# Attention and a gated MLP in one kernel: the late head pairs' scores as three products of split queries and keys

## The chip, the cores and the metric

The kernel runs on one core of a Trainium2 chip. The metric is the device time of one execution in microseconds (us). Times inside an execution come from one profiled run, counted from the start of its span.

## The reference

Eight batches of eight heads, 576 positions, 64 values per head. The attention mask is by blocks of 64: a query sees all keys of its own and of earlier blocks. The heads of a batch side by side are the 512 columns of the MLP's input, 4608 tokens in all.

```python
scores = 1/sqrt(64) * q @ k.T          # per batch and head, 576 x 576
scores = where(block_i >= block_j, scores, -1e9)
attn = exp(scores - max(scores)); attn /= sum(attn) + 1e-9
x = (attn @ v).transpose(0, 2, 1, 3).reshape(4608, 512)
h = x @ w_in                           # 512 x 2048
out = (h / (1 + exp(-1.702 * h))) @ w_out   # 2048 x 512
```

Everything comes in and goes out in float32; queries and keys are scaled so that the scores are spread widely.

## The kernel before, in words

**Attention.** Two heads make a pair; there are 32 pairs, four to a batch. A pair's two heads lie on partitions 0 to 63 and 64 to 127, so their score matmuls stand in different halves of the TensorE rows. `load` (L279) brings a pair's queries and keys into one tile, `raw`; `prep` (L303) turns both with two VectorE transposes into `qk` and, once `raw` is read, starts the load of the pair that follows. The 576 queries are five chunks (0 to 4) that see 64, 192, 320, 448 and 576 keys. `score` (L316) multiplies chunks 3 and 0, 2 and 1 in one block of four widths (448, 64, 320, 192) for each head; chunk 4 (384 and 192 wide) is multiplied behind the attention-times-values matmuls of the pair before, in `av` (L499 to L515). Each score is one float32 matmul (L340, L504, L511), all of them issued by the helper `mm` (L110). VectorE then adds the mask and takes the maximum (L389), ScalarE exponentiates (L396), GpSimd or VectorE divide by the sum (L415, L417).

**Early and late.** Pairs 0 to 7 are early: their weights are flipped on TensorE (L448). Pairs 8 to 31 are late: VectorE turns 32 x 32 blocks (L424, L429), and sixteen DMAs on the SyncE queue (L436) put the blocks in place. `settle` (L349) runs `prep` of the next pair after the scores of chunk 4.

**The MLP.** It works in tiles of 384 tokens, twelve in all (`moe`, L580). Each factor is a higher part, rounded to the reduced float32 (`F32R`), and a lower part, the rest; a product is three matmuls of parts (L617, L585). For each of 16 slices of the hidden width a tile has 12 matmuls into a bank `hp` (384 columns), the gate (`g`, `gh`, `gl`: L633, L634, L642, L643), and 9 matmuls of the slice before into the banks `acc0` to `acc2` (512 columns each). After the last slice, ScalarE copies each `acc` bank into an `osb` tile (L599), and a DMA on the SyncE queue writes it out (L601). The next tile's first matmul into an `acc` bank waits for the copy of that bank. There are three `osb` buffers.

**Weights.** They come as 64-bit words, and 32 pieces are merged (`begin`, `merge`) into a tile `wm`, of which ScalarE takes the higher part and GpSimd the lower (`split_weights`, L250, the subtraction is helper L84). The last pieces are staged in `osb` buffers and in a buffer tagged `e1`. The last piece is split while pair 7 is worked on.

**Order.** `ORDER` and its kin (L26 to L34) set the order in which a pair's steps are written; `advance` (L663) puts MLP matmuls between them. TensorE runs in just that order. On the other engines the order comes out of priorities. Each engine and the SyncE queue works in order: what waits holds up all behind it.

**Buffers.** A tag with one buffer holds one tile; the next tile of that tag waits until all readers of the old one are done.

Of the kernel before, what the change touches and what calls it, by code (L numbers as in the profile page):

```python
# [10 lines left out]
F32 = mybir.dt.float32  # L11
F32R = mybir.dt.float32r
U32 = mybir.dt.uint32
# [28 lines left out]
def attention_moe_kernel(  # L42
# [9 lines left out]
    nc = tc.nc  # L52
    B, H, S, D = q.shape
    DM, DF = w_in.shape
    P = 128
# [11 lines left out]
    K4 = 384  # L67

    sp = ctx.enter_context(tc.tile_pool(name="sp", bufs=1))
    d2 = ctx.enter_context(tc.tile_pool(name="d2", bufs=2))  # L70
    ps = ctx.enter_context(tc.tile_pool(name="ps", bufs=1, space=PSUM))

    def f(ap):
        return ap.bitcast(F32)

    def early(n):

        return n < 2 * HP
# [4 lines left out]
    def subtract(eng, out, in0, in1):  # L83
        eng.tensor_tensor(out=out, in0=in0, in1=in1, op=ALU.subtract)  # L84
# [3 lines left out]
    turns = {"n": 0, "bank": 0, "experts": False, "late": False}  # L88
# [20 lines left out]
    def mm(**kw):  # L109
        return tc.keep_in_program_order(nc.tensor.matmul(**kw))  # L110
# [14 lines left out]
    WC = 512  # L125
# [4 lines left out]
    def room(tag, shape, dt, name):  # L130
        return d2.tile(shape, dt, tag=tag, name=name, bufs=1)

    home = {}

    def weights(name, g):
# [36 lines left out]
    for i in range(NCH):  # L172
        w, o = BLK * (2 * i + 1), 2 * BLK * i * i
        es.append(flat[:, o : o + 2 * w].rearrange("p (h k) -> p h k", h=2))

    def width(i):
        return BLK * (2 * i + 1)
# [9 lines left out]
    for g in range(NG):  # L187
# [3 lines left out]
        for fc in range(FG):  # L191
            r = (g * FG + fc) * P
# [5 lines left out]
    def load_weights(upto):  # L198
        while conv["loaded"] < min(upto, len(pieces)):
            j = conv["loaded"]  # L200
            if j < 2 * len(places):
                if j % 2 == 0:
                    pair_of[j // 2] = room(places[j // 2], [P, 2, 2 * WC], U32, "words")
                at = [pair_of[j // 2][:, j % 2]]
            else:
                at = [
                    room("e1", [P, WC], U32, "wst") if j % 2 and x
                    else d2.tile([P, WC], U32, tag="osb", name="wst", bufs=3)
                    for x in range(2)
                ]  # L210
            n = 2 * WC // len(at)
            for x, w in enumerate(at):
                d = nc.sync.dma_start(out=w, in_=pieces[j][0][:, x * n : (x + 1) * n])
                if j < 3:
                    tc.keep_in_program_order(d)
            parts[j] = [
                (w.rearrange("p (c t) -> p c t", t=2), slice(x * n // 2, (x + 1) * n // 2))
                for x, w in enumerate(at)
            ]
            conv["loaded"] += 1  # L220
# [3 lines left out]
    bits, whole = {}, {}  # L224
# [48 lines left out]
    raw, qk = {}, {}  # L273
# [21 lines left out]
    def load_v(n):  # L295
        to = values(n)
        for hd, b, h in heads(n):
# [2 lines left out]
            )  # L300
            nc.sync.dma_start(out=to[0:BLK, hd, QC], in_=v[b, h, QC * P : S])

    def prep(n):  # L303

        tag = "e0" if early(n) and n % 2 else "qk"
        qk[n] = d2.tile([P, 2, S], F32, tag=tag, name="qk", bufs=1)
        for x in range(2):
            nc.vector.transpose(out=qk[n][:, x], in_=raw[n][:, x].rearrange("p c d -> p (c d)"))  # L308
        raw.pop(n)
        m = follower(n)  # L310
        if m is not None:
            load(m)
# [3 lines left out]
    def score(n, banks):  # L316

        turns["late"] = not early(n)
        if n not in stats:
            mx = d2.tile([P, NCH + 1, 2], F32, tag="mx", name="mx")  # L320
            sm = d2.tile([P, NCH, 2], F32, tag="sm", name="sm")
            stats[n] = (mx, sm)
        todo = []
        taken = 0
        for chunks in banks:

            part = []
            for lo, hi in ((0, 512),) if width(chunks[0]) <= 512 else ((0, 256), (256, S)):
                ss = []
                for _ in range(2):  # L330
                    taken += 1
                    ss.append(lent_bank() if taken == 1 and turns["late"] else bank())
                c = 0
                for i in chunks:
                    a, z = qrange(i)
                    w = min(hi, width(i)) - lo
                    for hd in range(2):
                        r = slice(hd * D, hd * D + D)

                        mm(  # L340
                            out=ss[hd][:, c : c + w], lhsT=qk[n][r, 0, a : a + P],
                            rhs=qk[n][r, 1, lo : lo + w], start=True, stop=True,
                        )
                        part.append((i, hd, lo, lo + w, ss[hd][0 : z - a, c : c + w]))
                    c += w
            todo.append(sorted(part, key=lambda x: (chunks[::-1].index(x[0]), x[2])))
        settle(n, banks, todo)
# [120 lines left out]
    def av(n):  # L468

        b, h = divmod(n, HP)  # L470
        before_av(n)
        if turns["late"]:
            o0, o = bank(), bank()
            cut = BLK + 2 * P
        else:
            o, o0 = bank(), bank()
            cut = BLK

        def place(q0):
            return (o0, q0) if q0 < cut else (o, q0 - cut)  # L480

        todo = []
        for i in range(1, NCH):
            bk, c = place((i - 1) * P + BLK)
            todo += [(bk, c, P, j, pw[:, :, SLOT[i] + j]) for j in range(i)]
            todo.append((bk, c + BLK, BLK, i, pw[:, 2:4, 9 + i]))
        todo.append((*place(0), BLK, 0, pw[:, 0:2, 10]))

        ends = [[x for x, y in enumerate(todo) if y[0] is bk] for bk in (o0, o)]
        for x, (bk, c, nn, j, w) in enumerate(todo):  # L490
            for hd in range(2):
                mm(
                    out=bk[hd * D : hd * D + D, c : c + nn].rearrange("d (a c) -> d a c", c=32),
                    lhsT=values(n)[:, hd, j], rhs=w[:, :, hd],
                    start=any(x == y[0] for y in ends), stop=any(x == y[-1] for y in ends),
                )
        m = n + 1
        rest = []
        if turns["late"] and m < NPAIR:  # L499
            own = [lent_bank(), bank()]  # L500
            a, z = qrange(4)
            for hd in range(2):
                r = slice(hd * D, hd * D + D)
                mm(  # L504
                    out=own[hd][:, 0:K4], lhsT=qk[m][r, 0, a : a + P],
                    rhs=qk[m][r, 1, 0:K4], start=True, stop=True,
                )
                rest.append((4, hd, 0, K4, own[hd][0 : z - a, 0:K4]))
            for hd, (bk, c) in enumerate(((o0, cut), (o, S - cut))):
                r = slice(hd * D, hd * D + D)  # L510
                mm(  # L511
                    out=bk[:, c : c + S - K4], lhsT=qk[m][r, 0, a : a + P],
                    rhs=qk[m][r, 1, K4:S], start=True, stop=True,
                )
                rest.append((4, hd, K4, S, bk[0 : z - a, c : c + S - K4]))  # L515
        c0 = (b % 2) * S
        nc.scalar.copy(out=xr[:, h, c0 : c0 + cut], in_=o0[:, 0:cut])
        nc.scalar.copy(out=xr[:, h, c0 + cut : c0 + S], in_=o[:, 0 : S - cut])
        nxt = follower(n)
        if nxt is not None:  # L520
            load_v(nxt)
        if rest:
            settle(m, [[4]], [sorted(rest, key=lambda x: x[2])])
# [56 lines left out]
    def moe():  # L580
        prev = None

        def second(state):
            g_hi, g_lo, fc, acc, t = state
            todo = [(c, ga, wb) for c in range(TILES[t][1] // P) for ga, wb in ((g_hi, "woh"), (g_hi, "wol"), (g_lo, "woh"))]  # L585
            if fc < NFC - 1:

                todo.sort(key=lambda x: x[1] is g_lo)
            begun = set()
            for x, (c, ga, wb) in enumerate(todo):  # L590
                last = ga is g_lo
                mm(
                    out=acc[c], lhsT=ga[:, c * P : (c + 1) * P], rhs=weights(wb, fc // FG)[:, fc % FG],
                    start=fc == 0 and c not in begun, stop=fc == NFC - 1 and last,
                )
                begun.add(c)
                if fc == NFC - 1 and last:
                    osb = d2.tile([P, DM], F32, tag="osb", name="osb", bufs=3)
                    nc.scalar.copy(out=osb, in_=acc[c])  # L599
                    r = TILES[t][0] + c * P  # L600
                    nc.sync.dma_start(out=out[r : r + P, :], in_=osb)  # L601
                if x % 3 == 2:
                    yield 650

        for t in range(NT):
# [6 lines left out]
            for fc in range(NFC):  # L612
# [8 lines left out]
                for cnt, (wa, xb, dc) in enumerate(terms):  # L621
                    mm(
                        out=hp[:, 0:tt], lhsT=weights(wa, fc // FG)[:, dc, fs], rhs=xb[:, dc, 0:tt],
                        start=cnt == 0, stop=cnt == 3 * NDC - 1,
# [111 lines left out]
```

## Time and profile before

| | us |
|---|---|
| Median of 3 runs | 1097.73 (1097.12 to 1099.45) |
| The profiled execution | 1097.56 |
| Its span | 1095.8 |
| TensorE matmuls busy | 1063.1 (97% of the span) |
| VectorE, ScalarE, GpSimd busy | 603.6, 499.3, 403.9 |

In a timeline a row is a start, a duration, an engine, a line, an operation and how many of them were merged into it; what stands in brackets is the idle time of the engine before the row and who ended it. PE is TensorE, PEld its weight loads, DVE VectorE, ACT ScalarE, POOL GpSimd, SPq the SyncE queue of DMAs. `bank<-qk` is a score matmul; a float32 matmul leaves two records, so eight records are four matmuls. Matmul durations overlap: what one costs is the distance from its start to the next start.

### The profile page before, as it was taken

How to read it: one execution, taken by the hardware profiler on the slowest of the kernel's cores; microseconds unless marked ns; L12 is line 12 of the kernel's file. 1: busy time of each engine (PE TensorE's matmuls, PEld its weight loads, DVE VectorE, ACT ScalarE, POOL GpSimd, SP SyncE). 2: the span in 40 equal slices, each digit the busy share in tenths (PEclk: the TensorE clock that was granted, in tenths of full speed). 3: DMA queues.
4: the chain of work that ended last, by engine and by line, in shares of the span. 5: the costliest groups of instructions: out<-in, count | busy, mean ns of one | idle time of the engine just before them, and what ended most of it. 6: DMA issues, size and time to landing. Idle time of an engine off the chain costs nothing.

```text
span 1095.8 us, 19944 instructions
## 1 busy us (share of the span) xinstructions
PE 1063.1 (97%) x6960; PEld 913.4 (83%) x6960; DVE 603.6 (55%) x1856; ACT 499.3 (46%) x1321; POOL 403.9 (37%) x509
## 2 busy tenths in 40 slices
PE   6869999999999999999999999999999999999998
PEld 4657777888888888888888888888888888999997
DVE  6786786765655656655655665655656655111111
ACT  5866776533443544533444543443544433322322
POOL 4666565423333333233333332333333233222222
PEclk8979999999999999999999999999999999999999
DMA  8734523433423444342434433233443321200000
GB/s 175 208 92 156 148 63 81 86 90 78 98 67 77 116 88 87 62 99 65 105 78 87 116 73 74 58 98 77 108 95 84 73 77 47 55 30 1 30 1 29
DMA packets 219364, 91.24 MB, mean 83 GB/s; under 512 B 197760, under 2 KB 197760, under 8 KB 219264
## 3 DMA queue, kind: packets, MB, share of 16 engines
q1 hardware_dynamic: 214528, 89.38, 34.5%
q10 hardware_dynamic: 4736, 0.59, 0.3%
q8 instruction: 55, 0.90, 0.3%
q14 instruction: 45, 0.37, 0.1%
HBM read 45.09 MB, written 9.44 MB: 50 GB/s over the span
## 4 chain that ended last, share of the span: by engine, by line
PE 89%; DVE 4%; ACT 2%; issue 2%; DMA 1%; SPq 1%; POOL 1%; POOLq 0%; DVEq 0%; ACTq 0%
PE hp L110 36%; PE acc L110 35%; PE bank L110 17%; PE bank L113 1%; ACT turned L396 1%; DMA raw<-in_k_dram 1%; SPq L290 1%; DVE wm L245 1%; DVE sm L405 1%; DVE qk L308 0%; DVE turned L389 0%; DVE e L389 0%; DMA words<-in_moe_w_out_dram 0%; DVE wm L240 0%; ACT e L396 0%
## 5 line engine op out<-in xcount | busy, mean ns | idle before, releaser
L84 POOL TENSOR_TENSOR gl<-g,gh 128x384 fp32r<-128x384 f32 x192 | 194.8, 1014 | 573.5 <-ACT gh L642 568.3
L634 DVE SCALAR_TENSOR_TENSOR g<-g,hp 128x384 f32<-128x384 f32 x192 | 104.9, 546 | 379.6 <-ACT g L633 379.5
L110 PE MATMUL hp<-xh,wih 128*128 128x384 f32 x768 | 260.6, 339 | 2.9 <-DVE g L634 2.2
L110 PE MATMUL hp<-xh,wil 128*128 128x384 f32 x768 | 258.1, 336 | 0.0
L110 PE MATMUL hp<-xl,wih 128*128 128x384 f32 x768 | 254.1, 338 | 0.1
L633 ACT ACTIVATE g<-hp 128x384 f32<-128x384 f32 x192 | 94.3, 491 | 312.8 <-PE hp L110 299.8
L110 PE MATMUL acc<-woh,gh 128*128 128x512 f32 x576 | 231.6, 402 | 0.0
L110 PE MATMUL acc<-wol,gh 128*128 128x512 f32 x576 | 226.7, 394 | 0.0
L110 PE MATMUL acc<-woh,gl 128*128 128x512 f32 x576 | 168.1, 393 | 0.5 <-POOL gl L84 0.5
L642 ACT CAST gh<-g 128x384 fp32r<-128x384 f32 x192 | 98.5, 513 | 141.0 <-DVE g L634 140.9
L110 PEld LDWEIGHTS hp<-xh,wih 128*128 128x128 f32 x768 | 144.3, 188 | 15.8 <-issue 3.3
L110 PEld LDWEIGHTS hp<-xh,wil 128*128 128x128 f32 x768 | 144.2, 188 | 7.7
L396 ACT ACTIVATE e<-e,mx 64x64 f32<-64x64 f32 (+4 forms) x240 | 131.9, 551 | 28.8 <-DVE mx L389 28.8
L110 PEld LDWEIGHTS hp<-xl,wih 128*128 128x128 f32 x768 | 143.6, 188 | 1.0 <-DVE xl L84 0.9
L110 PE MATMUL bank<-qk 64*128 64x192 f32 (+5 forms) x768 | 122.1, 431 | 13.9 <-DVE qk L308 11.1
L110 PEld LDWEIGHTS acc<-woh,gh 128*128 128x128 f32 x576 | 107.9, 187 | 28.1 <-issue 7.4
L415 POOL TENSOR_TENSOR e<-e,sm 64x64 f32<-64x64 f32 (+1 forms) x192 | 111.7, 611 | 51.7 <-DVE sm L410 40.7
L110 PEld LDWEIGHTS acc<-woh,gl 128*128 128x128 f32 x576 | 107.7, 188 | 25.8 <-POOL gl L84 1.8
L110 PEld LDWEIGHTS acc<-wol,gh 128*128 128x128 f32 x576 | 108.2, 188 | 16.5 <-issue 0.4
L110 PEld LDWEIGHTS bank<-qk 64*128 64x128 f32 x768 | 69.9, 194 | 53.5 <-issue 18.0
L389 DVE CUSTOM_DVE_ANT_0 e<-bank,mask 64x64 f32<-64x64 f32 (+4 forms) x240 | 92.8, 440 | 16.4 <-PE bank L110 15.2
L110 PEld LDWEIGHTS bank<-turned,vp 128*64 128x64 f32 x1800 | 85.4, 137 | 9.6 <-issue 6.6
(50 smaller groups left out, 985.7 us busy)
## 6 DMA issues: line engine op xcount, KB each, us to landing
turned<-turned SPq DMA_DIRECT2D x192, 80.0 KB, 2.1
turned<-turned SPq DMA_DIRECT2D x96, 112.0 KB, 2.2
raw<-in_q_dram SPq DMA_DIRECT2D x128, 72.0 KB, 2.4
out_dram<-osb SPq DMA_DIRECT2D x36, 256.0 KB, 2.2
raw<-in_k_dram SPq DMA_DIRECT2D x120, 72.0 KB, 2.3
turned<-turned SPq DMA_DIRECT2D x96, 88.0 KB, 2.1
words<-in_moe_w_in_dram SPq DMA_DIRECT2D x16, 512.0 KB, 5.7
vp<-in_v_dram SPq DMA_DIRECT2D x60, 128.0 KB, 2.5
```

The lines of the kernel that those rows point to most:

```text
L84: eng.tensor_tensor(out=out, in0=in0, in1=in1, op=ALU.subtract)
L110: return tc.keep_in_program_order(nc.tensor.matmul(**kw))
L113: return tc.keep_in_program_order(nc.tensor.transpose(**kw))
L245: nc.vector.scalar_tensor_tensor(out=z[:, c], in0=w[..., 0], scalar=29, in1=u[:, c], op0=ALU.logical_shift_right, op1=ALU.bitwise_or,)
L290: queue.dma_start(out=raw[n][r : r + 32, x], in_=src[b, h][:, c : c + 32].rearrange("(c p) d -> p c d", p=32),)
L389: nc.vector.tensor_tensor_reduce(out=e[0:m, hd, lo:hi], in0=s, in1=mk, op0=ALU.add, op1=ALU.min, scale=-0.125, scalar=3e38 if lo == 0 else ...
L396: nc.scalar.activation(out=e[0:m, hd], in_=e[0:m, hd], func=AF.Exp, scale=-1.0, bias=mx[0:m, i, hd : hd + 1], accum_out=sm[0:m, i, hd : hd ...
L405: x = nc.vector.tensor_scalar(out=c, in0=c, scalar1=1e-9, scalar2=2.0, op0=ALU.add, op1=ALU.mult)
L415: nc.gpsimd.tensor_tensor(out=x, in0=x, in1=sc.to_broadcast([m, width(i)]), op=ALU.mult)
L633: nc.scalar.activation(out=g, in_=hp[:, 0:tt], func=AF.Tanh, scale=1.702)
L634: nc.vector.scalar_tensor_tensor(out=g, in0=g, scalar=1.0, in1=hp[:, 0:tt], op0=ALU.add, op1=ALU.mult)
L642: nc.scalar.copy(out=gh, in_=g)
```

## The change

For late pairs `prep` now calls `prep_late`. VectorE still makes the two transposes, but into a buffer `qt` (in the tag `e1`) for the queries and back into `raw` for the keys. ScalarE casts each into a higher part (tags `wm` and `high`), and GpSimd subtracts, in two halves each, to get the lower part (`low`, tag `qk`). A score is then three matmuls in the reduced float32: higher by higher, lower by higher, higher by lower (`score_into`); the product of the two lower parts is left out. Early pairs are as before. The three `osb` buffers become the tags `osb0`, `osb1` and `high`; once a late pair has been scored, output copies use `osb0` and `osb1` alone, since `high` then holds the keys' higher part.

```diff
+    def out_room(shape, dt, name):
+        tags = ["osb0", "osb1"] + ([] if turns["late"] else ["high"])
+        outs["n"] += 1
+        return room(tags[outs["n"] % len(tags)], shape, dt, name)
...
+    def prep_late(n):
+        high[n] = [room(t, [P, S], F32R, "high") for t in ("wm", "high")]
+        low[n] = room("qk", [P, 2, S], F32R, "low")
+        for x in range(2):
+            whole = raw[n][:, 0].rearrange("p c d -> p (c d)") if x else room("e1", [P, S], F32, "qt")
+            nc.vector.transpose(out=whole, in_=raw[n][:, x].rearrange("p c d -> p (c d)"))
+            nc.scalar.copy(out=high[n][x], in_=whole)
+            for c in (slice(0, S // 2), slice(S // 2, S)):
+                subtract(nc.gpsimd, low[n][:, x, c], whole[:, c], f(high[n][x])[:, c])
+
+    def products(n, r, q0, k0, k1):
+        if early(n):
+            return [(qk[n][r, 0, q0 : q0 + P], qk[n][r, 1, k0:k1])]
+        (qh, kh), (ql, kl) = high[n], (low[n][:, 0], low[n][:, 1])
+        return [(x[r, q0 : q0 + P], y[r, k0:k1]) for x, y in ((qh, kh), (ql, kh), (qh, kl))]
+
+    def score_into(n, q0, banks, k0, k1):
+        todo = [products(n, slice(hd * D, hd * D + D), q0, k0, k1) for hd in range(2)]
+        for x in range(len(todo[0])):
+            for hd in range(2):
+                lhsT, rhs = todo[hd][x]
+                mm(out=banks[hd], lhsT=lhsT, rhs=rhs, start=x == 0, stop=x == len(todo[0]) - 1)
...
     def prep(n):
-        tag = "e0" if early(n) and n % 2 else "qk"
-        qk[n] = d2.tile([P, 2, S], F32, tag=tag, name="qk", bufs=1)
-        for x in range(2):
-            nc.vector.transpose(out=qk[n][:, x], in_=raw[n][:, x].rearrange("p c d -> p (c d)"))
+        if early(n):
+            qk[n] = room("e0" if n % 2 else "qk", [P, 2, S], F32, "qk")
+            for x in range(2):
+                nc.vector.transpose(out=qk[n][:, x], in_=raw[n][:, x].rearrange("p c d -> p (c d)"))
+        else:
+            prep_late(n)
...
-                    osb = d2.tile([P, DM], F32, tag="osb", name="osb", bufs=3)
+                    osb = out_room([P, DM], F32, "osb")
                     nc.scalar.copy(out=osb, in_=acc[c])
```

On TensorE the block of four score widths becomes twelve rows for each of the two heads; this is the block of pair 9, with the matmuls next to it, before:

```order
L110 MATMUL hp<-xl,wih 128x384
L110 MATMUL bank<-qk 128x448 [waits DVE_49]
L110 MATMUL bank<-qk 128x448 [waits PE_49]
L110 MATMUL bank<-qk 128x64 x2
L110 MATMUL bank<-qk 128x320 x2
L110 MATMUL bank<-qk 128x192 x2
L110 MATMUL acc_2351<-woh,gh 128x512 [waits Activation_49]
```

and now:

```order
L110 MATMUL bank<-high 128x448 [waits DVE_49]
L110 MATMUL bank<-high 128x448 [waits PE_49]
L110 MATMUL bank<-high,low 128x448 [waits Pool_49]
L110 MATMUL bank<-high,low 128x448
L110 MATMUL bank<-low,high 128x448 [waits Pool_49]
L110 MATMUL bank<-low,high 128x448
L110 MATMUL bank<-high 128x64 x2
L110 MATMUL bank<-high,low 128x64 x2
L110 MATMUL bank<-low,high 128x64 x2
L110 MATMUL bank<-high 128x320 x2
L110 MATMUL bank<-high,low 128x320 x2
```

All other TensorE rows stand in the order in which they stood.

On ScalarE, at the end of the fourth MLP tile, three output copies (`acc_4071` to `acc_4073`) stood together; a wait on DMAHW is a wait for a transfer. Before:

```order
L633 ACTIVATE g<-hp 128x384 [waits PE_49,Pool_49]
L599 COPY osb<-acc_4071 128x512 [waits DMAHW2_49,PE_49]
L642 CAST gh<-g 128x384 [waits DVE_49]
L599 COPY osb<-acc_4072 128x512 [waits DMAHW3_49,PE_49]
L599 COPY osb<-acc_4073 128x512 [waits DMAHW4_49,PE_49]
L633 ACTIVATE g<-hp 128x384 [waits PE_49,Pool_49]
L642 CAST gh<-g 128x384 [waits DVE_49]
```

and now (the same banks are `acc_4294` to `acc_4296`):

```order
L319 CAST high<-qt 128x576
L654 ACTIVATE g<-hp 128x384 [waits PE_49,Pool_49]
L620 COPY osb<-acc_4294 128x512 [waits PE_49]
L620 COPY osb<-acc_4295 128x512 [waits PE_49]
L663 CAST gh<-g 128x384 [waits DVE_49]
L654 ACTIVATE g<-hp 128x384 [waits PE_49,Pool_49]
L663 CAST gh<-g 128x384 [waits DVE_49]
L427 ACTIVATE e,sm<-e,mx 64x64 [waits DVE_49] x2
L427 ACTIVATE e,sm<-e,mx 128x448 [waits DVE_49] x2
L427 ACTIVATE e,sm<-e,mx 128x192 [waits DVE_49] x2
L427 ACTIVATE e,sm<-e,mx 128x320 [waits DVE_49] x2
L620 COPY osb<-acc_4296 128x512 [waits DMAHW1_49]
```

The third copy has moved behind the next pair's exponentials, and it waits for the transfer that the first copy's output takes. On the SyncE queue the three output transfers stand where they stood, behind the sixteen transfers of L436.

On GpSimd, where the weights end and the late pairs begin, before:

```order
L415 TENSOR_TENSOR turned<-turned,sm 128x576
L84 TENSOR_TENSOR wol<-wm,woh 128x512 [waits Activation_49] x2
L415 TENSOR_TENSOR e<-e,sm 64x64 [waits DVE_49,PE_49,Activation_49]
L415 TENSOR_TENSOR e<-e,sm 64x64 [waits Activation_49]
L415 TENSOR_TENSOR e<-e,sm 128x448 [waits DVE_49,DMAHW3_49,Activation_49,Pool_49]
```

and now:

```order
L84 TENSOR_TENSOR wol<-wm,woh 128x512 [waits Activation_49] x2
L84 TENSOR_TENSOR low<-qt,high 128x288 [waits Activation_49]
L84 TENSOR_TENSOR low<-qt,high 128x288
L84 TENSOR_TENSOR low<-raw,high 128x288 [waits DMAHW6_49,DMAHW5_49,DMAHW7_49,DMAHW4_49,Activation_49]
L84 TENSOR_TENSOR low<-raw,high 128x288
L446 TENSOR_TENSOR e<-e,sm 64x64 [waits DVE_49,PE_49,Activation_49]
```

The four subtractions of pair 8 have come between the last split of a weight and the pair's first division; the transposes of pair 8, which stood two pieces of weight earlier on VectorE, now follow the last merge.

More of the change, by code (lines that the diff above doesn't have):

```diff
@@ L131, in room @@
         return d2.tile(shape, dt, tag=tag, name=name, bufs=1)
+    outs = {"n": 0}
+    def out_room(shape, dt, name):
+        tags = ["osb0", "osb1"] + ([] if turns["late"] else ["high"])
+        outs["n"] += 1
+        return room(tags[outs["n"] % len(tags)], shape, dt, name)
     home = {}
@@ L207, in load_weights @@
                     room("e1", [P, WC], U32, "wst") if j % 2 and x
-                    else d2.tile([P, WC], U32, tag="osb", name="wst", bufs=3)
+                    else out_room([P, WC], U32, "wst")
                     for x in range(2)
@@ L301, in load_v @@
             nc.sync.dma_start(out=to[0:BLK, hd, QC], in_=v[b, h, QC * P : S])
-    def prep(n):
-        tag = "e0" if early(n) and n % 2 else "qk"
-        qk[n] = d2.tile([P, 2, S], F32, tag=tag, name="qk", bufs=1)
-        for x in range(2):
-            nc.vector.transpose(out=qk[n][:, x], in_=raw[n][:, x].rearrange("p c d -> p (c d)"))
+    high, low = {}, {}
+    def prep_late(n):
[18 more added lines that the diff above has]
+                mm(out=banks[hd], lhsT=lhsT, rhs=rhs, start=x == 0, stop=x == len(todo[0]) - 1)
+    def prep(n):
+        if early(n):
[4 more added lines that the diff above has]
+            prep_late(n)
         raw.pop(n)
@@ L336, in score @@
                     w = min(hi, width(i)) - lo
[L337 to L344, printed above, removed]
+                    score_into(n, a, [x[:, c : c + w] for x in ss], lo, lo + w)
+                    part += [(i, hd, lo, lo + w, ss[hd][0 : z - a, c : c + w]) for hd in range(2)]
                     c += w
@@ L501, in av @@
             a, z = qrange(4)
[L502 to L515, printed above, removed]
+            beside = [o0[:, cut : cut + S - K4], o[:, S - cut : S - cut + S - K4]]
+            for ss, lo, hi in (([x[:, 0:K4] for x in own], 0, K4), (beside, K4, S)):
+                score_into(m, a, ss, lo, hi)
+                rest += [(4, hd, lo, hi, ss[hd][0 : z - a]) for hd in range(2)]
         c0 = (b % 2) * S
```

## The prediction

> **What bounds the kernel.** I read the page first, then TensorE's timeline in one late period, then the ends of MLP tiles on the SyncE queue, where the change touches buffers.
>
> ```profile
> span 1095.8 us, 19944 instructions
> PE   6869999999999999999999999999999999999998
> PE 89%; DVE 4%; ACT 2%; issue 2%; DMA 1%; SPq 1%; POOL 1%; POOLq 0%; DVEq 0%; ACTq 0%
> ```
>
> TensorE is full from the fourth of 40 slices on, and the chain that ends last runs through it for 89%. In the late part a pair takes 31.6 us, and TensorE has no gap in it: what is added to or taken from TensorE there counts in full, and so does any wait that opens a gap. All else has room. The starts on TensorE in one period:
>
> ```profile
> 513.24 1.24 PE L110 MATMUL bank<-qk 64*128 64x384 f32 x8
> 514.41 0.50 PE L110 MATMUL acc<-woh,gh 128*128 128x512 f32 x1
> 514.75 0.39 PE L110 MATMUL acc<-wol,gh 128*128 128x512 f32 x1
> 514.98 0.40 PE L110 MATMUL acc<-woh,gh 128*128 128x512 f32 x1
> ...
> 522.53 0.33 PE L110 MATMUL hp<-xh,wil 128*128 128x384 f32 x1
> 522.70 0.34 PE L110 MATMUL hp<-xl,wih 128*128 128x384 f32 x1
> 522.97 2.11 PE L110 MATMUL bank<-qk 64*128 64x448 f32 x16
> 525.01 0.50 PE L110 MATMUL acc<-woh,gh 128*128 128x512 f32 x1
> ```
>
> Chunk 4's block lasts 514.41 - 513.24 = 1.17 us, the four-width block 525.01 - 522.97 = 2.04: 3.21 a pair, both heads together, 24 x 3.21 = 77 us in all. A reduced float32 matmul of 384 columns starts 0.17 after the last, one of 512 columns 0.23. Behind a change of shape the first takes 0.34 (514.41 to 514.75): 0.11 more, which I read as a load of 128 weight columns that nothing hides.
>
> **The products.** Removed: 3.21 a pair. Added: three products a width, whose pace no row shows below 384 columns or on half the rows. By 0.17 and 0.23, 448 columns take 0.20 and 320 take 0.145; at 64 and 192 I let the load of the next weights (0.11) set the pace. Four-width block: 3 x (0.20 + 0.11 + 0.145 + 0.11) = 1.70, with 0.2 for the two changes of shape 1.90, or 0.14 less. Chunk 4: 3 x (0.17 + 0.11) = 0.84, with 0.2 it is 1.04, or 0.13 less. 24 x 0.27 = -6 us. Bounds: with no floor from loads, 1600 x 3 columns at 0.17 / 384 us each are 2.1, with 0.4 for changes 2.5: 0.7 less a pair, or -16. If the nine narrow products took 0.19, the mean of a load's record (below), they would cost 9 x 0.08 = 0.7 more a pair: +11.
>
> ```profile
> L110 PEld LDWEIGHTS bank<-qk 64*128 64x128 f32 x768 | 69.9, 194 | 53.5 <-issue 18.0 <-DVE qk L308 11.9 <-DVE mx L389 4.1
> ```
>
> The Trainium skill ("FP8 and Floating Point Precision", section TensorE Precision Notes) counts a true float32 matmul as four passes and the reduced one as a single read cut to 22 bits. By that alone three products save a quarter of 3.21, an estimated -19 us; the exposed 0.11 in the trace speaks against so much at widths of 64 and 192.
>
> **The parts of queries and keys, in a steady period.** The transposes stay. Added are two casts and four subtractions:
>
> ```profile
> L84 POOL TENSOR_TENSOR gl<-g,gh 128x384 fp32r<-128x384 f32 x192 | 194.8, 1014 | 573.5 <-ACT gh L642 568.3 <-PE acc L110 5.2
> L84 POOL TENSOR_TENSOR wol<-wm,woh 128x512 fp32r<-128x512 f32 x16 | 20.5, 1284 | 7.9 <-ACT woh L254 7.8
> L254 ACT CAST woh<-wm 128x512 fp32r<-128x512 f32 x16 | 9.9, 620 | 8.8 <-DVE wm L245 8.7
> 521.56 1.02 POOL L84 TENSOR_TENSOR gl<-g,gh 128x384 fp32r<-128x384 f32 x1 [8.36 <-ACT gh L642]
> ```
>
> A cast of 576 columns is 0.67 us, a subtraction of 288 columns 0.81 by the line through 384 and 512: 3.2 a pair on GpSimd, which sits idle for 8.36 just there. They can start when chunk 4's products have left the old parts at 514.41. With ScalarE's other copies (some 0.7) between the casts the last part is ready by about 514.4 + 2.1 + 1.6 = 518.1, and TensorE wants it at 522.97: nothing, with 4.8 us of cover. The next load of `raw` now waits for the subtractions that read it, about 516.8, where it began at 517.3 before: no loss for the sixteen transfers behind it.
>
> **The handover to pair 8.** Here there is no cover.
>
> ```profile
> 184.85 0.62 ACT L254 CAST woh<-wm 128x512 fp32r<-128x512 f32 x1 [0.19 <-DVE wm L245]
> 185.55 1.27 POOL L84 TENSOR_TENSOR wol<-wm,woh 128x512 fp32r<-128x512 f32 x1 [1.52 <-ACT woh L254]
> 185.74 2.11 PE L110 MATMUL bank<-qk 64*128 64x448 f32 x16
> 187.78 0.44 PE L110 MATMUL hp<-xh,wih 128*128 128x384 f32 x1
> ```
>
> The higher part of pair 8's queries lies in `wm`, which GpSimd reads until 186.8. Cast until 187.5, four subtractions until 190.75; then the last product of the first width and the other three widths (1.4): the block ends at 192.2, not 187.78: +4.4. VectorE now waits for a division between two chunks' maxima, behind which a gate stands: up to 1.5 more. I take +5.
>
> **The ends of MLP tiles.** With two buffers the third output copy waits until the first output has landed, and on the queue that output can stand behind sixteen transfers. Of TensorE's rows only those are shown in which the next tile enters the third bank; the first fence is the fourth tile, the second the seventh:
>
> ```profile
> 458.00 1.07 ACT L599 COPY osb<-acc 128x512 f32<-128x512 f32 x2
> 459.13 10.71 SPq L436 DMA_DIRECT2D turned<-turned  x16
> 462.84 0.39 PE L110 MATMUL acc<-woh,gh 128*128 128x512 f32 x1
> 469.94 1.51 SPq L601 DMA_DIRECT2D out_dram<-osb  x3
> out_dram<-osb SPq DMA_DIRECT2D x36, 256.0 KB, 2.2
> ```
>
> ```profile
> 715.58 0.39 PE L110 MATMUL acc<-woh,gh 128*128 128x512 f32 x1
> 722.03 1.52 SPq L601 DMA_DIRECT2D out_dram<-osb  x3
> ```
>
> Before, all three banks were copied by 459.1, and the outputs lay in their buffers until the queue came to them: nobody waited. Now the third copy is ready 2.2 (landing) + 0.6 (copy) after the first issue: 472.7 against 462.84, or +9.9; 724.8 against 715.58, or +9.2. Nothing else can run on TensorE meanwhile, since its rows keep their order. Together +19.
>
> The first tile ends in the same way, right behind the handover:
>
> ```profile
> 203.00 1.95 SPq L290 DMA_DIRECT2D raw<-in_q_dram  x4
> 207.22 11.21 SPq L436 DMA_DIRECT2D turned<-turned  x16
> 209.62 0.39 PE L110 MATMUL acc<-woh,gh 128*128 128x512 f32 x1
> 218.53 1.50 SPq L601 DMA_DIRECT2D out_dram<-osb  x3
> ```
>
> By these 218.5 + 2.8 - 209.6 = +11.7. There `raw` was free with the transposes; now two casts (1.3) and four subtractions (3.2), partly beside each other, stand before its next load and so before the sixteen: up to +4. I take +14, between 11.7 and 16.
>
> At the third, sixth and ninth tile the output comes just after the sixteen; elsewhere the queue is free:
>
> ```profile
> 374.43 0.53 SPq L601 DMA_DIRECT2D out_dram<-osb  x1
> 376.40 0.39 PE L110 MATMUL acc<-woh,gh 128*128 128x512 f32 x1
> ...
> 539.14 1.98 SPq L601 DMA_DIRECT2D out_dram<-osb  x3
> ```
>
> 374.4 + 2.8 - 376.4 = 0.8, at most 2.4 for three; I take +1.5. Where the queue is free (539.14, right behind the first copy) the third is late by a microsecond and TensorE has other work: nothing. At the very end it has none:
>
> ```profile
> 1090.96 1.97 ACT L599 COPY osb<-acc 128x512 f32<-128x512 f32 x3 [1.67 <-PE acc L110]
> 1091.58 1.71 SPq L601 DMA_DIRECT2D out_dram<-osb  x3
> ```
>
> The last copy began at about 1092.35 and would begin at 1091.6 + 2.2 = 1093.8: +1.4.
>
> **The clock.** TensorE idling for 9 us or more will find its clock lowered:
>
> ```profile
> 57.40:60.80 3.40, 1.03 (x11) 0.96 (x12) 2.94 (x6) 1.15 (x2) 2.54 (x4) 1.00 0.01 2
> 60.80:64.20 3.40, 0.47 (x3) 0.09 (x1) 2.05 (x4) 1.76 (x5) 2.96 (x3) 0.51 0.82 132
> 71.10:74.50 3.40, 3.40 (x23) 2.85 (x24) 3.01 (x9) 3.40 (x11) 1.98 (x4) 0.50 0.19 78
> 74.50:77.90 3.40, 2.69 (x53) 2.55 (x50) 2.27 (x3) 2.52 (x7) 3.40 (x5) 1.00 0.02 5
> ```
>
> (PEclk is the third number from the end of each row.) After two stretches with TensorE mostly idle the clock was 0.50 until 74.5, ten microseconds after work had come back at about 64. At half clock half of that is lost: between 0 and 5 for each of the three long waits; I take 2.5 each, +7.5. The Trainium skill ("TensorE: Matmul & The Clock Gate", Part 1) has the clock back after one busy window of 3.4 us; by it the three would cost an estimated 5, and the row of 74.5, which shows a slower return, speaks against so little.
>
> **The sum.** -6 + 5 + 19 + 14 + 1.5 + 1.4 + 7.5 = +42.4 on the profiled execution's 1097.56, which stands 0.02% from the median of 1097.73: 1140. The bounds of the terms give -16 + 4.4 + 18 + 11.7 + 0.5 + 1 + 0 = +20, or 1117, and +11 + 6 + 20 + 16 + 2.4 + 1.5 + 15 = +72, or 1170; not all will fall on one side.
>
> **Rivals.**
> Not slower: the third copy's wait is hidden. It would take the output to land before TensorE enters the third bank, so an issue by 460.0 at the fourth tile; the sixteen transfers (10.71 us at one queue's pace) would have to stand behind it. Then what is left is -6 + 5 + 1.4: 1098, from 1088 to 1100 with the products' and the handover's bounds. For it: in other tiles the queue is free. Against: the queue's order is unchanged and was busy until 469.9, 722.0 and 218.5. 0.06, half of it faster.
> Narrow products run at float32's pace: (2.04 - 1.17) / 448 = 1.94 ns a column. Then 448 narrow columns x 3 cost 2.6 in place of 1.0 a pair: 24 x 1.6 = +39, 1179. No reduced row narrower than 384 speaks for or against. 0.08.
> The two heads, which run side by side in float32 (both heads' sixteen records in one block of 2.04), run one after the other in reduced float32: 24 x 2.54 = +61, 1201. The rows are the same halves, so 0.03.
>
> **The numbers.** The forecast has 0.83. 1122 to 1162 leaves out little of it and all of the rivals: about 0.8. A measurement here can tell 0.2%, some 2 us. Faster 0.03 and same 0.02 come from the first rival, with 0.01 of slower; slower is 0.95 in all.
>
> **What would show it.** Right: third output copies at the first, fourth and seventh tile that start 2 to 3 us after the first output's issue, TensorE idle for 9 to 15 us before the third bank at those places, released by the copy; a clock below 1 behind each; pair 8's block ending 4 to 6 later, with waits on GpSimd; late blocks of 1.9 and 1.04. Wrong: blocks of 3 us or more, or third copies that come with the others.

## The result, and the profile after

| | before | after |
|---|---|---|
| Median | 1097.72 us (4 runs, 1097.12 to 1099.45) | 1147.89 us (4 runs, 1147.40 to 1148.42) |
| Profiled execution, its span | 1097.56, 1095.8 | 1147.42, 1145.6 |
| Mean granted clock | 0.990 | 0.972 |

The ratio is 1.045, with a 95% interval from 1.044 to 1.047. The page of the changed kernel, first TensorE in 40 slices, then the chain of waits:

```profile
span 1145.6 us, 20751 instructions
PE   5879998599999999979999999969999999999998
PE 80%; ACT 5%; DVE 5%; DMA 3%; SPq 3%; issue 2%; POOL 2%; POOLq 0%; DVEq 0%; ACTq 0%
```

TensorE carries 80% of the chain that ends last, where it carried 89%. The holes are in slices 8, 18 and 27 of 40: the ends of the first, fourth and seventh MLP tile. The waits of TensorE by what ended them (total, times, longest) name them:

```profile
PE acc L110 <- ACT osb L620: 39.3, 6, 13.9
```

This row is not in the kernel before. Six waits for an output copy make 39.3 us of the 49.8 by which the span grew. The end of the fourth tile, in the timelines of ScalarE, of the SyncE queue and of TensorE:

```profile
478.56 1.28 ACT L620 COPY osb<-acc 128x512 f32<-128x512 f32 x2
480.79 10.06 SPq L467 DMA_DIRECT2D turned<-turned  x16
490.94 3.15 SPq L622 DMA_DIRECT2D out_dram<-osb  x3
493.15 0.59 ACT L620 COPY osb<-acc 128x512 f32<-128x512 f32 x1 [4.08 <-DMA out_dram<-osb]
493.79 0.80 PE L110 MATMUL acc<-woh,gh 128*128 128x512 f32 x1 [8.74 <-ACT osb L620]
```

Two banks are copied at once. The first output then stands behind the sixteen transfers until 490.94, lands 2.2 us later, the third copy runs, and TensorE enters the third bank at 493.79 after 8.74 idle. The first tile has the same rows, with a longer gap:

```profile
226.34 3.18 SPq L622 DMA_DIRECT2D out_dram<-osb  x3
228.57 0.59 ACT L620 COPY osb<-acc 128x512 f32<-128x512 f32 x1 [9.41 <-DMA out_dram<-osb]
229.21 0.79 PE L110 MATMUL acc<-woh,gh 128*128 128x512 f32 x1 [13.90 <-ACT osb L620]
```

At the third, sixth and ninth tile the output goes out sooner, and the copy is late all the same. The SyncE queue, ScalarE and TensorE at the third:

```profile
395.18 4.23 SPq L622 DMA_DIRECT2D out_dram<-osb  x3
396.94 0.49 ACT L654 ACTIVATE g<-hp 128x384 f32<-128x384 f32 x1 [1.12 <-POOL gl L84]
...
398.47 0.58 ACT L620 COPY osb<-acc 128x512 f32<-128x512 f32 x1
399.10 0.50 PE L110 MATMUL acc<-woh,gh 128*128 128x512 f32 x1 [2.28 <-ACT osb L620]
```

The first output takes 2.2 to land, so it has landed by about 397.4, and the third copy starts 1.1 after that. It has no wait of its own: it stands in ScalarE's order behind the next gate, and that gate waits for GpSimd. The handover, on TensorE and GpSimd:

```profile
187.22 0.47 PE L110 MATMUL bank<-high 64*128 64x448 f32 x2 [2.35 <-ACT high L319]
188.27 0.47 PE L110 MATMUL bank<-high,low 64*128 64x448 f32 x2 [0.58 <-POOL low L84]
189.77 0.74 PE L110 MATMUL bank<-low,high 64*128 64x448 f32 x2 [1.03 <-POOL low L84]
```

The first width's three products wait one after the other for their parts, as GpSimd makes them. And a steady block of four widths, TensorE alone:

```profile
259.91 0.47 PE L110 MATMUL bank<-high 64*128 64x448 f32 x2
260.21 0.36 PE L110 MATMUL bank<-high,low 64*128 64x448 f32 x2
260.42 0.36 PE L110 MATMUL bank<-low,high 64*128 64x448 f32 x2
260.62 0.19 PE L110 MATMUL bank<-high 64*128 64x64 f32 x2
260.65 0.28 PE L110 MATMUL bank<-high,low 64*128 64x64 f32 x2
260.76 0.28 PE L110 MATMUL bank<-low,high 64*128 64x64 f32 x2
...
261.80 0.50 PE L110 MATMUL acc<-woh,gh 128*128 128x512 f32 x1
```

The block takes 261.80 - 259.91 = 1.89 us, where the float32 block took 2.04. From product to product it is some 0.20 at 448 columns (260.21, 260.42, 260.62) and 0.11 at 64 columns (260.65, 260.76).

### The profile page after: what moved, and what is told of

Read it like the earlier page. It is cut to its first block, busy times and chain, and to the rows that moved or that the text cites. A ratio compares the mean times of both kernels' runs of the same rounds, so it can differ in the third digit from the quotient of the medians.

```text
span 1145.6 us, 20751 instructions
## 1 busy us (share of the span) xinstructions
PE 1068.5 (93%) x7248; PEld 938.4 (82%) x7248; DVE 598.9 (52%) x1856; ACT 523.6 (46%) x1369; POOL 481.7 (42%) x605
## 4 chain that ended last, share of the span: by engine, by line
PE 80%; ACT 5%; DVE 5%; DMA 3%; SPq 3%; issue 2%; POOL 2%; POOLq 0%; DVEq 0%; ACTq 0%
PE hp L110 33%; PE acc L110 32%; PE bank L110 14%; SPq L467 2%; ACT e L427 1%; PE bank L113 1%; DMA vp<-in_v_dram 1%; DMA out_dram<-osb 1%; ACT turned L427 1%; DVE turned L455 1%; DVE g L655 1%; DVE wm L252 1%; DMA words<-in_moe_w_out_dram 1%; DVE turned L420 1%; DMA raw<-in_k_dram 0%
## 5 line engine op out<-in xcount | busy, mean ns | idle before, releaser
L110 PE MATMUL acc<-woh,gh 128*128 128x512 f32 x576 | 234.1, 406 | 39.3 <-ACT osb L620 39.3
L436 DVE TENSOR_SCALAR sm<-sm 128x2 f32<-128x2 f32 (+1 forms) x160 | 63.2, 395 | 61.2 <-ACT e L427 55.2
L110 PE MATMUL bank<-turned,vp 128*64 128x128 f32 (+1 forms) x1800 | 89.6, 257 | 1.6 <-ACT turned L481 1.6
```

Of the source, the lines that this page charges most:

```text
L436: x = nc.vector.tensor_scalar(out=c, in0=c, scalar1=1e-9, scalar2=2.0, op0=ALU.add, op1=ALU.mult)
```

## The experiments

The theory is that the products are a small gain, and that the loss is the wait of the third output copy: with two buffers it waits for a transfer that stands in the SyncE queue behind sixteen others. The first rival is that the products, with the casts and subtractions that make their parts, cost the time; others are the clock and the handover to pair 8.

**Two buffers alone** (two_buffers). The kernel before, in which late output copies have two buffers; nothing is split.

```diff
+        tags = ["osb0", "osb1"] + ([] if turns["late"] else ["osb2"])
...
-                    osb = d2.tile([P, DM], F32, tag="osb", name="osb", bufs=3)
+                    osb = out_room([P, DM], F32, "osb")
```

> The kernel before with one change: once a late pair has been scored, output copies have two buffers in place of three. Scores stay in float32, nothing else moves. Theory of the buffers: the third copy of an MLP tile waits for the first output, which stands behind the sixteen transfers on the SyncE queue. From the rows of before the waits are 11.7 at the first tile (there are no subtractions here that hold up the sixteen), 9.9 and 9.2 at the fourth and seventh, some 2.3 each at the third, sixth and ninth as the changed kernel showed, 1.3 at the end, and about 8 of lost clock behind them: 1097.7 + 11.7 + 19.1 + 6.8 + 1.3 + 8 = 1145, from 1138 to 1148. Theory of the products (the score products, their casts and subtractions cost the time): 1098 to 1100, since none of them is here.

Measured: 1141.20 us, 1.040 of before (1.038 to 1.041). Its waits on TensorE:

```profile
PE acc L110 <- ACT osb L606: 34.5, 6, 10.8
```

The wait comes with the buffers, without one split product: 34.5 us idle, +43 in all. That is most of the 50, and the theory of the products is out. The first tile's wait is 10.8 here and 13.9 in the changed kernel. Here the sixteen start 2.6 before TensorE reaches the bank, in the changed kernel 0.6 after it: 3.2 later. The prediction had up to 4 for the subtractions that stand before the next load of `raw`, and the traces bear it out: that load is issued at 205.05 here, when the second transpose ends (205.03), and at 211.69 in the changed kernel, when the last subtraction ends (211.66).

**No third output** (skip_third). The changed kernel, in which late tiles but the last leave out the third copy and its write.

```diff
-                if fc == NFC - 1 and last:
+                if fc == NFC - 1 and last and (c < 2 or not turns["late"] or t == NT - 1):
```

> The changed kernel without the copy and the write of the last 128 tokens of each MLP tile but the last one, once a late pair has been scored: that part of the output is left out. Outputs stay on the SyncE queue behind the sixteen transfers. Theory of the buffers: with two copies a tile and two buffers nobody waits for the queue, and the time is that of act_queue within 2 us: 1100, from 1096 to 1104. If what holds TensorE is the queue of sixteen transfers in another way (the next weights, raw or the blocks), or the products: 1130 or more.

Measured: 1100.60 us, 1.0023 of before (1.0011 to 1.0035). Everything else of the change is in this kernel: the split products, their preparation, the handover, two buffers. Together that costs 2.5 us, in a kernel that also has less to copy and to write.

**Outputs from another queue** (act_queue, and before_act_queue as a control). One line of the changed kernel:

```diff
-                    nc.sync.dma_start(out=out[r : r + P, :], in_=osb)
+                    nc.scalar.dma_start(out=out[r : r + P, :], in_=osb)
```

> The changed kernel with one line changed: output tiles are written from ScalarE's queue of DMAs, where no sixteen transfers stand ahead of them. Two buffers, split scores and all else stay. Theory of the buffers: the third copy waits only for some 2.2 us of one transfer, and the waits of TensorE for output copies (39.3 us) go, and the lost clock behind them (about 8.8 of 12) with them: 1147.9 - 39.3 - 8.8 = 1100, from 1096 to 1104. What is left above 1097.7 is then the handover (5 to 6, and up to 3.4 of lost clock) less the products (6). Theory of the products: the queue does not matter, 1140 or more.

Measured: 1105.36 us, 1.0072 (1.0057 to 1.0088), just above the expected range. Of the 39.3 us this is left:

```profile
PE acc L110 <- ACT osb L620: 2.4, 3, 0.9
```

So the place in the queue made the wait. The median is 5 above the run without the third output. The profiled spans differ by 3.0 (1101.8 against 1098.8), of which three waits of 0.7 to 0.9, at the third, sixth and ninth tile, make 2.4; the rest is not traced. The control is the same line changed in the kernel before.

> The kernel before with one line changed: output tiles are written from ScalarE's queue. A control for the runs above: with three buffers nobody waited for the SyncE queue, so nothing is to be gained: within 2 us of the kernel before. If writing outputs there is worth something by itself (the sixteen transfers land earlier) it is faster by more; if ScalarE pays for issuing them, slower by up to 36 x 0.34 = 12.

Measured: 1112.16 us, 1.0127 (1.0110 to 1.0143): 14 slower, which is more than the 12 that the expectation allowed for the issues on ScalarE, and it has another cause. The ScalarE row is an output's issue, the SyncE row the last three of the sixteen transfers of the fifth tile's pair; then TensorE:

```profile
546.09 0.34 ACTq L601 DMA_DIRECT2D out_dram<-osb  x1
548.14 1.78 SPq L436 DMA_DIRECT2D turned<-turned  x3
552.11 1.11 PE L110 MATMUL bank<-turned,vp 128*64 128x128 f32 x20 [3.18 <-DMA turned<-turned]
```

Thirteen of the sixteen were issued by 536.6; the fourteenth waits until 548.14, just when the output issued at 546.09 has had some 2 us to land. In the program, transfers signal their end on eight semaphores taken in turn, over both queues, and each waits for the last user of its semaphore. The output and the fourteenth transfer have the same one. So a transfer on one queue waited for one on the other, which could not be issued before its copy was made. Four waits of TensorE for turned blocks make 10.4 us; the kernel before has none.

**The buffer of the turned queries** (third_in_e1, queue_and_e1). The changed kernel, with the buffer of `qt` as a third output buffer.

```diff
-        tags = ["osb0", "osb1"] + ([] if turns["late"] else ["high"])
+        tags = ["osb0", "osb1"] + (["e1"] if turns["late"] else ["high"])
```

> The changed kernel with one line changed: while late, output copies take osb0, osb1 and the buffer of qt (tag e1), which holds the turned queries only for a few microseconds of each period. Outputs stay on the SyncE queue behind the sixteen transfers. Theory of the buffers: a third buffer is all that was missing, the waits of 39.3 us and the clock behind them go, and the time is that of the run without the third output: 1100.6, from 1098 to 1103. If the next pair's turned queries now wait for the third output in that queue, TensorE waits for the scores in place of the copies: 1115 or more. If only the queue's length counts: 1140.

Measured: 1147.80 us, 1.046 (1.044 to 1.048), no gain. The third copies at the first, fourth and seventh tile now come with the others, and the wait has moved. TensorE's waits, then VectorE and TensorE at the first tile:

```profile
PE hp L110 <- DVE mx L420: 20.2, 3, 9.7
PE acc L110 <- ACT osb L620: 12.8, 3, 4.3
```

```profile
228.23 1.16 DVE L455 STREAM_TRANSPOSE turned<-e 128x128 f32<-128x128 f32 x4 [4.63 <-DMA turned<-turned]
229.62 0.62 DVE L420 CUSTOM_DVE_ANT_0 e<-bank,mask 128x448 f32<-128x448 f32 x1 [0.23 <-DMA out_dram<-osb]
230.40 0.66 PE L110 MATMUL hp<-xh,wih 128*128 128x384 f32 x1 [9.68 <-DVE mx L420]
```

The buffer holds chunk 3's exponentials too, which I had overlooked when I named the turned queries. So chunk 3's maxima now wait for the output, and in VectorE's new order they stand behind transposes that wait for the sixteen; TensorE needs the bank that they read. At the third, sixth and ninth tile TensorE waits 4.3, since the third copy waits until those exponentials are read. The expectation's second case came true in its time, but by chunk 3's exponentials and not by the turned queries.

> The run third_in_e1 with the output tiles written from ScalarE's queue: three buffers again while late (osb0, osb1 and qt's), and no sixteen transfers ahead of an output. Theory: in third_in_e1 the wait had only moved, to VectorE's transpose into qt, behind the third output in the SyncE queue; with a quick queue neither the copy nor the transpose waits, and the time is that of the run without the third output, 1100.6, from 1098.5 to 1103. If the order that VectorE has now is itself the cost (maxima behind the transpose), it stays above 1115.

Both edits together. Measured: 1132.10 us, 1.031 (1.030 to 1.033): above the 1115 of the expectation's second case, but not by the maxima that it named. The waits at the first, fourth and seventh tile are gone; at the third, sixth and ninth TensorE waits 23.2 for copies, since these wait for the readers of the exponentials:

```profile
388.50 0.58 ACT L620 COPY osb<-acc 128x512 f32<-128x512 f32 x1 [4.84 <-DVE turned L455]
```

**Outputs first** (outputs_first). Two buffers and the SyncE queue as in the changed kernel; the copies and outputs get a higher priority in the order.

```diff
-                    osb = out_room([P, DM], F32, "osb")
+                    with tc.high_priority(offset=300 if turns["late"] else 0):
+                        osb = out_room([P, DM], F32, "osb")
```

> The changed kernel with its two output buffers and its SyncE queue; the only edit is a priority that sets a tile's copies and outputs earlier in the order, so that at the first, fourth and seventh tile the outputs stand among the loads of raw, ahead of the sixteen transfers, and at the third, sixth and ninth the third copy stands ahead of the next gate. Theory: what made two buffers dear was only the place of the first output in the queue. The third copy then waits 2 to 3 us for one transfer and TensorE idles for at most a microsecond a tile: 1147.9 - 39.3 - 8.8 + up to 6 = 1100 to 1106. If the outputs now hold the loads of raw and the sixteen transfers (some 3 us later) and TensorE waits for those, as it waited for the turned blocks in before_act_queue: 1110 or more.

Measured: 1127.61 us, 1.027 (1.025 to 1.028). The second case, larger than I put it. No wait for a copy is left at the first, fourth and seventh tile, but at the second the SyncE queue and TensorE show this:

```profile
275.01 6.25 SPq L467 DMA_DIRECT2D turned<-turned  x10
291.50 1.33 SPq L623 DMA_DIRECT2D out_dram<-osb  x2
292.88 1.16 SPq L467 DMA_DIRECT2D turned<-turned  x2
294.92 0.34 SPq L623 DMA_DIRECT2D out_dram<-osb  x1
295.30 2.41 SPq L467 DMA_DIRECT2D turned<-turned  x4
299.71 1.55 PE L110 MATMUL bank<-turned,vp 128*64 128x128 f32 x14 [5.38 <-DMA turned<-turned]
```

The outputs now stand among the sixteen, and the queue is idle from 281.3 to 291.5 until the first copy is made. It is the same wait from the other side: six of the sixteen behind an output, in place of the output behind the sixteen. Six waits for turned blocks make 19.3 us.

**The handover.** Three kernels leave pair 8 in float32, on top of third_in_e1, queue_and_e1 and outputs_first. The same line is changed in `products` and in `prep`, with `FIRST = 8`.

```diff
-        if early(n):
+        if n <= FIRST:
```

> The run third_in_e1, with pair 8's scores left in one float32 product as before, so that no part has to be made while GpSimd still splits the last weights; pairs 9 to 31 are split. If the handover costs what its waits show (3.4 of idle TensorE, 3.4 at half clock behind it, less the 0.27 that pair 8's products gave), this run is 4.5 to 6 below third_in_e1: 1095 where that one gives 1100.6, from 1093.5 to 1096.5, below the kernel before. If the handover costs nothing, because later steps have room to catch up, the two are within 1 us. If pair 9 takes over the wait, they are within 2.

> The run queue_and_e1 with pair 8's scores left in float32. The handover priced alone: 3.9 of idle TensorE and up to 3.4 of lost clock less 0.27, so 5 to 7 below queue_and_e1: 1094.5 where that one gives 1100.6, from 1093 to 1097, at or below the kernel before. If the first outputs of the late part lend it the rest of the 9.1 that the same step gave between third_in_e1 and pair8_float32, it is 9 below, 1091.5. If pair 9 takes over the wait, less than 2 below.

> The run outputs_first with pair 8's scores left in float32. The handover's price, which was 9.1 between third_in_e1 and pair8_float32 and 3.6 between queue_and_e1 and queue_e1_pair8, is measured once more where no long wait follows it: 5 to 7 by its own waits (3.9 idle, up to 3.4 at half clock, less 0.3). So 1095 to 1099 where outputs_first gives 1102: level with the kernel before, or faster if the third copies cost nothing.

Measured: 1138.73, 1128.49 and 1126.20 us, that is 9.1, 3.6 and 1.4 below their partners; 1.038 (1.036 to 1.039), 1.028 (1.026 to 1.029) and 1.026 (1.025 to 1.028) of before. The differences of medians disagree, because what follows the handover moves too, and the place of pair 7's end differs by some 3 us between runs. A distance in the trace is steadier: from pair 7's last TensorE transposes to pair 9's block. First the kernel before, then the changed kernel:

```profile
182.86 1.20 PE L113 MATMUL bank<-ident,turned 128*128 128x128 f32 x9 [0.78 <-POOL turned L415]
...
206.57 2.11 PE L110 MATMUL bank<-qk 64*128 64x448 f32 x16
```

```profile
181.91 1.20 PE L113 MATMUL bank<-ident,turned 128*128 128x128 f32 x9 [0.78 <-POOL turned L446]
...
212.20 0.47 PE L110 MATMUL bank<-high 64*128 64x448 f32 x2
```

That is 23.71 and 30.29; in queue_e1_pair8 it is 24.91 (183.11 to 208.02). The other kernels lie within 0.4 of one of these, by what they do with pair 8, but for the next one. The handover costs 6.6, of which 5.4 go when pair 8 stays in float32.

The fourth run moves pair 8's first scores two places later in `HANDOVER`, on top of act_queue (`"B C - 3+0/2+1 ..."` becomes `"B C - - - 3+0/2+1 ..."`).

> The run act_queue with the first scores of pair 8 written two places later in the order of the handover, so that MLP matmuls stand before them while GpSimd subtracts. If the handover's loss is TensorE waiting for the subtractions (5 to 6, and up to 3.4 of lost clock behind that), it goes: 1100 less 5 to 9, so 1091 to 1095, faster than before. If the later scores only push the wait on to the maxima and exponentials of pair 8, which then miss their place, it stays at 1100 or above.

Measured: 1102.98 us, 1.0053 (1.0038 to 1.0068), 2.4 below act_queue, and above the 1100 of the expectation's second case. TensorE's idle time at this place falls only from 3.4 to 2.7. In part that is because the casts are late by a gate that now stands ahead of them on ScalarE:

```profile
187.39 0.49 ACT L654 ACTIVATE g<-hp 128x384 f32<-128x384 f32 x1 [1.48 <-PE hp L110]
187.78 0.67 ACT L319 CAST high<-qt 128x576 fp32r<-128x576 f32 x1
```

**One product** (one_product). pair8_float32 with the higher by higher product alone.

> The run pair8_float32 with only the product of the two higher parts for pairs 9 to 31; the two products with a lower part are left out, the lower parts are still made. If the narrow products of 64 and 192 columns go at the pace of a weight load (0.11), a pair loses 2 x (0.20 + 0.11 + 0.145 + 0.11) + 2 x (0.17 + 0.11) = 1.69, 23 pairs 38.9. If columns alone count (1600 at 0.17 / 384 each), a pair loses 2 x 0.71 = 1.42, 23 pairs 32.6. If every product costs a third of the block with its changes of shape, it is 2/3 x 2.93 = 1.95, 23 pairs 44.9. If the preparation sets the pace, so that the products are hidden, nothing.

Measured: 1140.76 us, 1.039 (1.037 to 1.041), 2.0 above pair8_float32. The block itself did shrink as the loads' pace says, from 1.89 to 0.75:

```profile
443.69 0.82 PE L110 MATMUL bank<-high 64*128 64x448 f32 x8 [0.41 <-DVE g L656]
444.44 0.50 PE L110 MATMUL acc<-woh,gh 128*128 128x512 f32 x1
```

With chunk 4's 0.46 that is 1.21 a pair, against 2.92 for three. The kernel does not show it, because TensorE now waits in nearly every period for the gate's steps on ScalarE, VectorE and GpSimd (8.4 for `gl`, 6.7 for `gh`, 10.0 for `g`; in pair8_float32 0.3, none and 4.6), and the long waits grew from 15.6 and 12.8 to 25.7 and 15.7. I had named the preparation as what could hide it; whether the preparation or the scheduler's new order does it was not separated.

## Why the prediction was right, and which terms were off

Its direction, its mechanism and its range held: 1147.89 against 1140 (1122 to 1162). The terms, in us:

| Term | predicted | in the trace of after |
|---|---|---|
| Products, 24 pairs | -6 | -6 (steady period 31.59 to 31.34) |
| Preparation in a steady period | 0 | 0 (no wait for `high` or `low` but at pair 8) |
| Handover | +5 | +6.8 (the 6.6 above, and pair 8's 0.27) |
| First tile | +14 | +13.9 |
| Fourth and seventh tile | +19 | +18.6 (8.74 + 9.86) |
| Third, sixth and ninth tile | +1.5 | +6.8 (2.28 + 2.27 + 2.27) |
| End | +1.4 | +1.3 |
| Clock behind the waits for copies | +7.5 | +9.6 (8.8 at half clock, 0.8 not traced) |

The right column adds to 51; pair 7's steps lay 0.9 earlier in this run, which leaves 50.1 against the 49.8 of the span. The forecast came out 8 low because the handover, the third, sixth and ninth tile and the clock were all priced too low.

**The products** came out by the rows: 1.89 and 1.03 for the two blocks, predicted 1.90 and 1.04. A narrow product goes at 0.11, which I read as an exposed weight load, so 64 columns cost more than half of 448. The Trainium skill's count of passes ("FP8 and Floating Point Precision", TensorE Precision Notes) had given -19; the measured -6 decides against it at these widths. A pair's 2.92 also rules out the two rivals that made the products dearer, by 1.6 and by 2.54 a pair.

**The long waits** were right to half a microsecond in their sums, and two_buffers shows that they belong to the buffers. One by one the fourth tile's 8.74 was priced at 9.9 and the seventh's 9.86 at 9.2; that the two errors cancel is luck. The rival in which the wait is hidden failed as the prediction said: the queue was busy until 490.9.

**The third, sixth and ninth tile** are the term that failed by most. The prediction priced the transfer (0.8, at most 2.4 for the three) and took the copy to start when it lands. The copy starts later than that, behind a gate in ScalarE's order, as the rows of 395.18 to 399.10 show: of the 2.28 some 1.2 is the transfer and its copy, and 1.1 the gate. The order quoted ahead of the prediction had shown such a move for the fourth tile only.

**The handover** was priced by its waits alone: 2.35 + 0.58 + 1.03 = 4.0 idle, a little under the 4.4 that it had for the block. The rest, near 3 us, is half clock behind them, which was not charged there: the clock was at half from 189.6 to 196.5. It put the term above its bound of 6.

**The clock** was mis-sized both ways. Behind the three long waits it took less than the 7.5 that I charged. The mean clock, third number from the end, behind the fourth tile's:

```profile
490.00:493.40 3.40, 0.00 (x0) 0.00 (x0) 1.96 (x7) 0.25 (x1) 1.39 (x3) 0.50 0.70 227
493.40:496.80 3.40, 3.01 (x8) 2.53 (x9) 2.50 (x7) 0.34 (x1) 0.00 (x0) 0.50 0.20 77
496.80:500.20 3.40, 3.40 (x19) 3.10 (x18) 0.55 (x1) 0.80 (x2) 0.00 (x0) 0.99 0.02 5
```

Work is back at 493.79 and the clock at 496.8: half of 3.0 is lost, 1.5; at the seventh tile 1.5 again, at the first, where the clock came back 4.8 after the work, 2.4. That is 5.4. By the Trainium skill ("TensorE: Matmul & The Clock Gate", Part 1) the estimate was 5, and the trace comes close to it; I had weighed the row of 74.5 against it. Short waits that I had charged nothing cost more: behind the sixth and the ninth tile's a whole stretch of 3.41 is at half clock, 1.7 each. With the 5.4 that is 8.8. The five periods that end with the third, fourth, sixth, seventh and ninth tile hold 25.4 idle and are 32.6 longer than undisturbed ones; the clock explains 6.4 of the 7.2 between, and 0.8 stays open.

**No version beat the kernel before.** The nearest, without the third output, is 2.5 above it, and by the distance above 5.4 of the handover could still come off it: an estimate of some 1095. That would need a third buffer that nothing else uses; it was not tried.

## What to carry to other kernels

A buffer that is taken away is priced by how long its content lies waiting on a queue, not by the transfer: here a transfer of 2.2 us held its buffer for up to 19. Moved to another buffer or place, that wait met a new one. Moved to another queue it all but went here, while the same line made a new wait in the kernel before. In these traces an instruction or a transfer that is not ready holds up all behind it on its engine or queue; so read what stands ahead of and behind the moved instruction on its engine and its queue. A gain of 0.25 us a period needs few such waits to be lost.

## What the runs showed of the hardware

A short gap lowers the clock or does not, by where it falls. The mean clock around the third tile's gap (396.82 to 399.10) and the sixth's (660.49 to 662.77):

```profile
394.50:397.90 3.40, 2.32 (x13) 1.80 (x11) 0.72 (x2) 1.49 (x3) 2.41 (x4) 1.00 0.61 205
397.90:401.30 3.40, 2.20 (x11) 1.98 (x12) 3.37 (x12) 1.00 (x2) 1.01 (x1) 1.00 0.20 77
```

```profile
660.70:664.10 3.40, 1.33 (x6) 1.11 (x7) 2.94 (x10) 1.40 (x3) 1.01 (x1) 1.00 0.28 106
664.10:667.50 3.40, 3.40 (x13) 3.40 (x12) 2.04 (x4) 0.00 (x0) 0.00 (x0) 0.50 0.05 17
```

Both gaps are 2.3 us. Split over two stretches, which stay busy for 2.32 and 2.20 of 3.4, the first costs no clock; the second leaves 1.33 in one stretch, and the next 3.4 us run at half clock, 1.7 lost. The stretches at half clock behind pair 8 and behind the copies last from 3.41 to 17.07 us, all multiples of 3.41. The Trainium skill ("TensorE: Matmul & The Clock Gate", Part 1) has a free-running window of 3413 ns, and the trace agrees. A gap shorter than the window was enough here. Cut the traces of all fourteen kernels into such stretches: in one at full clock that a half-clock stretch followed, TensorE was busy for at most some 1.83 us (before_act_queue, from 24.78), and in one that another at full clock followed for at least 1.58 (pair8_float32, from 383.81). So it took about half a stretch without work, and no whole one.
